# Two gated state-space convolutions on one core: the last two blocks' final sums taken apart, one accumulation moved into TensorE, and a new order table

## The chip, the cores and the metric

The kernel runs on one core of a Trainium2 chip. Its five engines work at the same time, each through its own queue of instructions: TensorE (PE) multiplies matrices into eight PSUM banks, VectorE (DVE) and ScalarE (ACT) work on elements and read PSUM, GpSimd (POOL) works on elements in SBUF and issues DMAs, SyncE (SP) only issues DMAs. An instruction waits on semaphores for what it needs, and all that stand behind it in its queue wait with it. The metric is the time of one execution on the device in microseconds (us); less is better.

## The reference

For an input `u` of 2048 positions and 512 channels, two independent state-space layers A and B each build a convolution kernel of 2048 taps per channel from 128 complex modes, convolve `u` with it, and a gate mixes the two results.

```python
def _A_ref(u, log_A_real, A_imag, C_real, C_imag, log_dt, D_skip):
    dt = jnp.exp(log_dt)
    A = -jnp.exp(log_A_real) + 1j * A_imag
    C = (C_real + 1j * C_imag) * dt[:, None]
    P = jnp.exp((A * dt[:, None])[:, :, None] * pos[None, None, :])
    K = 2.0 * jnp.einsum("dn,dnl->dl", C, P).real
    Kf = jnp.fft.rfft(K, L2)
    Uf = jnp.fft.rfft(u_t, L2)
    y = jnp.fft.irfft(Uf * Kf[None, :, :], L2)[:, :, :L]
    return y + u * D_skip[None, None, :]
...
g = _sigmoid((x * gate_w).sum(-1, keepdims=True))
return g * a + (1 - g) * b
```

All is computed in float32 here, with float16 pairs for the phases alone.

## The kernel before

**Units and blocks.** The 512 channels of A and B together make 64 units of 16 channel rows. A unit `u` builds its taps. PE adds up phases (`phase`, L508: eight float16 products, the only ones whose weights are loaded by instructions of their own); ACT takes sines and cosines; POOL multiplies powers of the decay (`grid0`, `grid1`, L524); DVE multiplies both (`cos_minus` to `one_sin`, L547 to L567); PE sums over the modes (`modes`, L575: 32 products of 32x64, run as 64 products in the trace, since a float32 product is two there, each with a weight load before it). So a float32 product of the program costs four PE instructions. ACT and DVE store the taps as `ks` (`keep`, `skip`).

Four units make a block `b` (16 blocks, 0 to 15). Two units' taps go through a first small transform (`first_k`, L597) and ACT copies it into `xall` (`keep_x`, L604). Then the block has eight middle transforms (`s2`, L634), each followed by two DVE products with the input's spectrum `v` (`products`, L645). The first product stays in the block's own part of `xall`; the second lands in `t2`, a part of `xall` that all blocks share, with real and imaginary rows exchanged. Four DMAs on POOL's queue add `t2` to the block's part, halves of the partitions exchanged (`add_products`, L675). Then four inverse transforms (`inverse`, L685: four products with the 128x128 table `mi` each), which ACT copies into `z` (`keep_z`, L691).

**Final sums.** Four blocks are a group `sb`. When all four have their `z`, four final sums (`final`, L707) multiply it with the gated table `eg`: 64 products each, with 32 weight columns and 64 moving columns, 16 for each of the group's four blocks. A sum fills two PSUM banks; ACT (in the last group ACT and DVE) copies them out (L718), and SP sends each of the two to DRAM, 128 KB. The gate is formed once, early: four sums over channels (`gate`, L737), a sigmoid, and a product on `eg`.

**What sets the order.** All operations are recorded in a list `ops`; the table `ORDER` says in which order they are issued, and each engine is held to that order by dependencies. A second table, `SLOTS`, says which of the eight PSUM banks each result takes. Both were written out beforehand; no rule of the program decides anything. Since a bank must be read before it is written again, `SLOTS` adds waits of its own.

**The end.** Behind the last unit stand, on PE: the first transforms of block 15, its eight middle transforms, block 14's inverses, block 15's inverses (which need the accumulating DMAs), and the last group's four final sums.

Of the kernel before, what the change touches and what calls it, by code (L numbers as in the profile page):

```python
# [11 lines left out]
F32 = mybir.dt.float32  # L12
# [7 lines left out]
M = 32  # L20
Q = 64
# [165 lines left out]
]  # L187


# [773 lines left out]
```

## Time and profile before

| | |
|---|---|
| times of three runs | 508.79, 510.26, 770.3 us; median 510.26 |
| profiled execution | 509.48 us, its span 507.6 us |
| mean granted TensorE clock | 0.95 |
| PE, DVE, ACT, POOL busy | 86%, 79%, 79%, 66% of the span |
| PE instructions | 12144 products, 12144 weight loads |

The span runs from the first to the last instruction; the time of the same execution is 1.9 us longer. A row of the profile names the line, the engine, the operation and the tiles (written tile, arrow, read tiles); what stands in brackets at its end is how long the engine was idle ahead of it and what ended that. "issue" means that nothing the profile shows was waited for. PE's busy time is of pipelined products and is no measure of how well the array is used. Line numbers are those of the kernel before.

### The profile page before, as it was taken

The numbers are of one execution on the slowest core, as the hardware profiler recorded it, in microseconds if no ns is written. First come the engines' busy times: TensorE is split into PE (matmuls) and PEld (weight loads), VectorE is DVE, ScalarE is ACT, GpSimd is POOL, SyncE is SP. The second block draws the span as 40 slices with busy tenths as digits, with TensorE's granted clock in tenths as the row PEclk, the third lists the DMA queues.
The fourth block names the chain that finished last, engine by engine and source line by source line (L and its number), as shares of the span: only waits on it lengthen the run. The fifth ranks groups of instructions, "written<-read, shape, count | busy, mean of one in ns | idle before, by whom it ended". The sixth has DMA issues, their size and how long they took to land.

```text
span 507.6 us, 27312 instructions
## 1 busy us (share of the span) xinstructions
PE 437.3 (86%) x12144; PEld 354.7 (70%) x12144; DVE 398.5 (79%) x860; ACT 399.3 (79%) x801; POOL 335.0 (66%) x320
## 2 busy tenths in 40 slices
PE   5886799896989889998999898968998888986774
PEld 5763664665858667876788677847786767876774
DVE  6498695999989999998789898859699788872401
ACT  4798799895999999799997997869979596843220
POOL 1499989996999899677784856554729662622200
PEclk9998899998999999999999999989999999989755
DMA  4537829026260633246513723271607352445312
GB/s 128 182 114 197 301 90 226 7 54 137 46 147 4 128 96 65 45 81 146 107 23 74 173 44 67 76 153 32 142 4 149 87 87 54 76 109 90 72 40 76
DMA packets 31349, 49.87 MB, mean 98 GB/s; under 512 B 10112, under 2 KB 16768, under 8 KB 31232
## 3 DMA queue, kind: packets, MB, share of 16 engines
q1 hardware_dynamic: 26112, 31.35, 21.5%
q0 software_dynamic: 5120, 16.78, 19.9%
q8 instruction: 95, 1.56, 1.3%
q14 instruction: 22, 0.18, 0.1%
HBM read 17.18 MB, written 5.77 MB: 45 GB/s over the span
## 4 chain that ended last, share of the span: by engine, by line
PE 49%; ACT 15%; DVE 13%; issue 9%; POOL 8%; DMA 5%; DVEq 0%; SPq 0%; ACTq 0%; POOLq 0%
PE ps L634 15%; PE psi L685 9%; PE pk L575 7%; PE p0s L508 6%; PE pf L707 5%; PE ps L597 5%; POOL f L524 4%; DMA xall<-xall 3%; ACT xall L604 3%; DVE xall L645 2%; ACT z L691 2%; PE psu L597 2%; DVE f L563 2%; ACT p0c L514 2%; DVE f L547 1%
## 5 line engine op out<-in xcount | busy, mean ns | idle before, releaser
L524 POOL TENSOR_TENSOR f<-bas 128x1024 f32<-128x1024 f32 (+1 forms) x128 | 204.7, 1645 | 71.4 <-PE pk L575 43.9
L634 PE MATMUL ps<-xall,gk 128*64 128x64 f32 (+1 forms) x1728 | 115.9, 260 | 13.7 <-issue 7.4
L634 PEld LDWEIGHTS ps<-xall,gk 128*64 128x64 f32 (+1 forms) x1728 | 105.4, 164 | 27.1 <-issue 12.3
L645 DVE TENSOR_TENSOR xall<-ps,v 128x256 f32<-128x256 f32 x256 | 95.1, 416 | 26.7 <-PE ps L634 24.3
L675 POOL DMA_DIRECT2D xall<-xall x64 | 61.5, 1119 | 50.6 <-ACT z L691 16.9
L575 PE MATMUL pk<-f,f 128*32 128x64 f32 x4096 | 72.4, 222 | 10.8 <-issue 3.6
L685 PE MATMUL psi<-mi,xall 128*128 128x128 f32 x512 | 71.9, 292 | 5.7 <-DMA xall<-xall 2.5
L575 PEld LDWEIGHTS pk<-f,f 128*32 128x32 f32 x4096 | 62.3, 111 | 19.1 <-issue 11.8
L685 PEld LDWEIGHTS psi<-mi,xall 128*128 128x128 f32 x512 | 64.0, 200 | 15.3 <-ACT z L691 5.0
L551 DVE TENSOR_TENSOR f<-f,p0c 128x512 f32<-128x512 f32 x64 | 43.6, 682 | 17.0 <-ACT p0c L520 14.2
L691 ACT COPY z<-psi 128x512 f32<-128x512 f32 x64 | 37.3, 604 | 22.0 <-PE psi L685 21.8
L508 PE MATMUL p1s<-cph,ones 64*128 64x512 f16 x128 | 49.5, 387 | 3.4 <-DVE ks L585 1.4
L563 DVE TENSOR_TENSOR f<-f,p1c 128x512 f32<-128x512 f32 x64 | 43.7, 683 | 10.3 <-ACT p1c L520 8.6
L597 PE MATMUL ps<-w,ks 64*64 64x64 f32 x2048 | 41.4, 226 | 11.6 <-issue 4.8
L508 PE MATMUL p0s<-cph,ones 64*128 64x512 f16 x128 | 49.6, 388 | 1.2 <-DVE f L567 0.5
L597 PEld LDWEIGHTS ps<-w,ks 64*64 64x64 f32 x2048 | 35.9, 139 | 20.9 <-issue 7.2
L508 PE MATMUL p0s<-cph,rot 64*128 64x512 f16 x128 | 49.2, 385 | 0.5 <-issue 0.5
L508 PE MATMUL p1s<-cph,rot 64*128 64x512 f16 x128 | 49.1, 384 | 0.0
L567 DVE TENSOR_TENSOR f<-f,p1s 128x512 f32<-128x512 f32 x64 | 43.6, 682 | 2.8 <-ACT p1s L517 0.8
L604 ACT COPY xall<-ps 128x512 f32<-128x512 f32 x64 | 37.3, 611 | 10.8 <-PE ps L597 10.7
L547 DVE TENSOR_TENSOR f<-f,p0c 128x512 f32<-128x512 f32 x64 | 43.6, 682 | 2.3 <-ACT p0c L520 1.2
L559 DVE SCALAR_TENSOR_TENSOR f<-f,p0s 128x512 f32<-128x512 f32 x64 | 43.4, 681 | 1.8 <-ACT p0s L517 1.0
(121 smaller groups left out, 794.4 us busy)
## 6 DMA issues: line engine op xcount, KB each, us to landing
xall<-xall POOLq DMA_DIRECT2D x64, 256.0 KB, 5.2
v<-v SPq DMA_DIRECT2D x64, 128.0 KB, 3.8
uraw<-in_us SPq DMA_DIRECT2D x16, 256.0 KB, 4.9
z<-in_ut SPq DMA_DIRECT2D x16, 256.0 KB, 5.9
out_dram<-ot SPq DMA_DIRECT2D x32, 128.0 KB, 1.9
par<-in_par SPq DMA_DIRECT2D x8, 256.0 KB, 3.7
gk<-in_gk SPq DMA_DIRECT2D x4, 512.0 KB, 7.1
eg<-in_eg SPq DMA_DIRECT2D x4, 512.0 KB, 7.0
```

The lines of the kernel that those rows point to most:

```text
L508: PE.matmul(ps, w[h : h + 64], cph[h : h + 64, j], start=j == 0, stop=j == 3, tile_position=(h, 0))
L524: G.tensor_tensor(o.rearrange("p k (a b) -> p k a b", b=8), x[:, :, hi : hi + n].unsqueeze(3).to_broadcast([128, 16, n, 8]), x[:, :, lo : ...
L547: V.tensor_tensor(f0[:, 0, :, 0:32], f0[:, 1, :, 0:32], half(u, p0c[u], True), OP.mult)
L563: V.tensor_tensor(f[:, 0], f[:, 1], p1c[u], OP.mult)
L575: PE.matmul(pk[32 * kd : 32 * kd + 32, i, :], f1[:, p, 4 * i + kd, :], f0[:, p, 4 * i + kd, :], start=p == 1, stop=p == 0, tile_position=( ...
L597: PE.matmul(ps[h][64 * ri : 64 * ri + 64, n, :], x[r], w1[r, ri, r], start=True, stop=True, tile_position=(64 * h, 64 * ri),)
L604: S.copy(o, pxs[key][h])
L634: PE.matmul(ps[h : h + w, j, 0:n], gk[:, k, h : h + w], xall[:, x0:x1, 2 * k : 2 * k + 2], start=True, stop=True, tile_position=(0, h),)
L645: V.tensor_tensor(k.rearrange("p x (k t) -> p k x t", t=2), p2s[b, g][:, :, 0:64].rearrange("p k (x t) -> p k x t", t=2), vv.unsqueeze(3). ...
L675: G.dma_start(out=xk(b)[o, s], in_=t2[t, s], accum_op=OP.add)
L685: PE.matmul(ps[:, i, :], xk(b)[:, x : x + 2, :].rearrange("p x k -> p (x k)"), mi, start=True, stop=True)
L691: S.copy(z[:, :, d0 : d0 + 4], pis[b, g].rearrange("p i r -> p r i"))
```

## The change

1. **The last group's final sums are split.** `final` for the last group now takes the first two of its blocks alone (12 and 13; 32 moving columns instead of 64), so it can stand before the last blocks are done. The last two blocks (14 and 15) get sums of their own, `last`: two of them, 64 products each, with 64 weight columns (two positions at once) and 64 moving columns (the same two positions). Of each 64x64 result only the two quarters where the positions agree are read. `eg` is laid out with the position next to the column for that.
2. **Copies and outputs follow.** `last_keep` copies each bank in four pieces of 32 partitions, on ACT and on DVE; the last group's outputs have a layout of their own (`out_at`) that the host code puts back in place.
3. **Block 15 has no accumulating DMAs.** Its `inverse` multiplies its own part of `xall` with `mi` and the shared part `t2` with `mt`, a copy of `mi` with the two halves of its rows exchanged, and adds both in PSUM: eight products instead of four.
4. **Eight unread products** (`hold`): 128x512, written to a bank that nobody reads.
5. **`ORDER` and `SLOTS` are other tables**, from the first entries to the last.

```diff
-    0, 19, 20, 21, 22, 23, 1, 2, 24, 45, 26, 25, 28, 29, 27, 30, 40, 41, 5, 74, 75, 32, 31, 78,
...
+    2480, 2493, 2483, 2481, 2482, 2477,
...
+    mt = const.tile([128, 128], F32, name="mt")
...
-    eg = const.tile([128, Q, 2, M], F32, name="eg")
+    eg = const.tile([128, 2, Q, M], F32, name="eg")
...
+    def hold(n):
+        PE.matmul(bank("pw"), ident, gk[:, 0:4, :].rearrange("p k x -> p (k x)"), start=True, stop=True)
...
     def inverse(b, g):
         pis[b, g] = ps = bank("psi", (128, 4, 128))
         for i in range(4):
             x = 2 * (4 * g + i)
-            PE.matmul(
-                ps[:, i, :], xk(b)[:, x : x + 2, :].rearrange("p x k -> p (x k)"), mi, start=True, stop=True
-            )
+            parts = [(xk(b), mi), (t2, mt)] if b == nblk - 1 else [(xk(b), mi)]
+            for n, (t, w) in enumerate(parts):
+                PE.matmul(
+                    ps[:, i, :], t[:, x : x + 2, :].rearrange("p x k -> p (x k)"), w,
+                    start=n == 0, stop=n == len(parts) - 1,
+                )
...
     def final(sb, j):
-        z0 = 0 if sb % 2 == 0 else NB
-        ps = [bank(f"pf{dp}")[:, 0:256].rearrange("p (a b) -> p a b", a=4) for dp in range(2)]
+        z0 = 0 if sb % 2 == 0 else 3 * NB if sb == nsb - 1 else NB
+        w = 32 if sb == nsb - 1 else 64
+        ps = [bank(f"pf{dp}")[:, 0 : 4 * w].rearrange("p (a b) -> p a b", a=4) for dp in range(2)]
...
+    def last(i):
+        ps = [bank(f"pl{dp}").rearrange("p (a q b) -> p a q b", a=8, q=2) for dp in range(2)]
+        for r4 in range(8):
+            for n in range(2):
+                for h in range(2):
+                    r = 32 * i + 4 * r4 + 2 * h
+                    for dp in range(2):
+                        rows = slice(64 * dp, 64 * dp + 64)
+                        PE.matmul(
+                            ps[dp][64 * h : 64 * h + 64, r4], eg[rows, n, r : r + 2, :],
+                            z[rows, 64 * n + r : 64 * n + r + 2, NB : 3 * NB],
+                            start=n == 0, stop=n == 1, tile_position=(64 * dp, 64 * h),
+                        )
+        pfs[i] = ps
+
+    def last_keep(i, dp):
+        ots[i, dp] = work.tile([128, 256], F32, name="ot", tag="ot", bufs=4)
+        o = ots[i, dp].rearrange("p (a b) -> p a b", a=8)
+        copy = V.tensor_copy if dp else S.copy
+        for rq in range(4):
+            rows = slice(32 * rq, 32 * rq + 32)
+            copy(o[rows], pfs[i][dp][rows, :, rq % 2])
...
-        if b >= 0:
+        if 0 <= b < nblk - 1:
             for h in range(2):
                 for x in range(2):
                     op("ya", add_products, b, h, x)
...
+    for h in range(2):
+        op("lm", dma, mt[64 * h : 64 * h + 64], a["mi"][64 - 64 * h : 128 - 64 * h])
...
-            if b % 4 == 3:
+            if b % 4 == (1 if b // 4 == nsb - 1 else 3):
...
+    for n in range(8):
+        op("wt", hold, n)
+    for i in range(2):
+        op("fl", last, i)
+        for dp in range(2):
+            op("fm", last_keep, i, dp)
+            op("fn", last_out, i, dp)
```

The end of the order on PE, before. `ps` is a middle transform's bank, `psi` an inverse's, `pf` a final sum's; a final sum is 64 rows, of which the first two and the last two stand here, and the three sums between them are left out.

```order
L634 MATMUL ps_9160<-xall,gk 64x64 x8
L634 MATMUL ps_9169<-xall,gk 64x64 x8
L685 MATMUL psi<-mi,xall 128x128 x32
L707 MATMUL pf_9240<-z,eg 32x64
L707 MATMUL pf_9241<-z,eg 32x64
...
L707 MATMUL pf_9456<-z,eg 32x64
L707 MATMUL pf_9457<-z,eg 32x64
L959 UNCONDITIONAL_BRANCH
```

The same place in the change, from the end of block 15's last inverse on (`mi` and `mt` in turn), with `pw` the unread bank and `pl` the last sums:

```order
L694 MATMUL psi<-mi,xall 128x128
L694 MATMUL psi<-mt,xall 128x128
L293 MATMUL pw<-gk,ident 128x512
L750 MATMUL pl_9548<-z,eg 64x64
L750 MATMUL pl_9549<-z,eg 64x64
...
L750 MATMUL pl_9627<-z,eg 64x64
L750 MATMUL pl_9628<-z,eg 64x64
L293 MATMUL pw<-gk,ident 128x512 x5
L1018 UNCONDITIONAL_BRANCH
```

All four inverses of block 15 stood together with block 14's (32 products in one row) ahead of four final sums; now two last sums follow the last inverse, one unread product stands between, and five stand behind everything. The other two unread products stand further ahead, one behind a final sum of the third group and one behind the last unit's phases.

The copies on ACT tell how inverses and early final sums alternate. `z` is the copy of an inverse, `ot` that of a final sum. Before:

```order
L604 COPY xall<-ps_9052 128x8x64
L718 COPY ot<-pf_8880 128x256
L691 COPY z<-psi 128x128x4 x11
L718 COPY ot<-pf_9240 128x256
L718 COPY ot<-pf_9309 128x256
L718 COPY ot<-pf_9384 128x256
L718 COPY ot<-pf_9456 128x256
```

In the change:

```order
L701 COPY z<-psi 128x128x4 x3
L733 COPY ot<-pf_9300 128x128
L733 COPY ot<-pf_9301 128x128
L701 COPY z<-psi 128x128x4 x2
L733 COPY ot<-pf_9382 128x128
L733 COPY ot<-pf_9383 128x128
L701 COPY z<-psi 128x128x4
L733 COPY ot<-pf_9463 128x128
L701 COPY z<-psi 128x128x4
L733 COPY ot<-pf_9464 128x128
L763 COPY ot<-pl_9548 32x256 x4
L763 COPY ot<-pl_9627 32x256 x4
```

Eleven inverses in a row and then the sums have become rounds of an early sum's two copies and one or two inverses' copies. On POOL the program ended with eight accumulating DMAs, for blocks 14 and 15:

```order
L524 TENSOR_TENSOR f_8747<-bas 128x512
L524 TENSOR_TENSOR f_8799<-bas 128x512
L524 TENSOR_TENSOR f_8854<-bas 128x1024
L675 DMA xall<-xall 64x1024 x8
L959 UNCONDITIONAL_BRANCH
```

Now the same place has four, those of block 14:

```order
L530 TENSOR_TENSOR f_8703<-bas 128x512
L530 TENSOR_TENSOR f_8764<-bas 128x512
L530 TENSOR_TENSOR f_8882<-bas 128x1024
L681 DMA xall<-xall 64x1024 x4
L1018 UNCONDITIONAL_BRANCH
```

More of the change, by code (lines that the diff above doesn't have):

```diff
@@ L707, in final @@
                         PE.matmul(
-                            ps[dp][32 * rq : 32 * rq + 32, r4, :], eg[rows, r, n, :],
-                            z[rows, 64 * n + r, z0 : z0 + 64],
+                            ps[dp][32 * rq : 32 * rq + 32, r4, :], eg[rows, n, r, :],
+                            z[rows, 64 * n + r, z0 : z0 + w],
                             start=n == 0, stop=n == 1, tile_position=(64 * dp, 32 * rq),
@@ L713, in final, with out_at, last_out @@
             pfs[sb, j, dp] = ps[dp]
+    def out_at(i, w):
+        o = out[nsb - 1].rearrange("j d p c -> (j d p c)")
+        return o[128 * i : 128 * (i + w)].rearrange("(p c) -> p c", p=128)
     def final_keep(sb, j, dp):
         ots[sb, j, dp] = work.tile([128, 256], F32, name="ot", tag="ot", bufs=4)
-        copy = V.tensor_copy if sb == nsb - 1 and dp else S.copy
-        copy(ots[sb, j, dp], pfs[sb, j, dp].rearrange("p a b -> p (a b)"))
+        w = 128 if sb == nsb - 1 else 256
+        S.copy(ots[sb, j, dp][:, 0:w], pfs[sb, j, dp].rearrange("p a b -> p (a b)"))
     def final_out(sb, j, dp):
-        dma(out[sb, j, dp], ots[sb, j, dp])
+        if sb == nsb - 1:
+            dma(out_at(128 * (2 * j + dp), 128), ots[sb, j, dp][:, 0:128])
+        else:
+            dma(out[sb, j, dp], ots[sb, j, dp])
+    def last(i):
[19 more added lines that the diff above has]
+            copy(o[rows], pfs[i][dp][rows, :, rq % 2])
+    def last_out(i, dp):
+        dma(out_at(1024 + 256 * (2 * i + dp), 256), ots[i, dp])
     psg = {}
@@ L744, in gate_e @@
     def gate_e(j):
-        e = eg[:, 16 * j : 16 * j + 16]
+        e = eg[:, :, 16 * j : 16 * j + 16]
         g = psg[j].rearrange("p (r m) -> p r m", m=M)
-        V.tensor_tensor(e, e, g.unsqueeze(2).to_broadcast([128, 16, 2, M]), OP.mult)
+        V.tensor_tensor(e, e, g.unsqueeze(1).to_broadcast([128, 2, 16, M]), OP.mult)
     def load_e(j):
-        dma(eg[:, 16 * j : 16 * j + 16], a["eg"][:, 16 * j : 16 * j + 16])
+        dma(eg[:, :, 16 * j : 16 * j + 16], a["eg"][:, :, 16 * j : 16 * j + 16])
     def batch(i):
@@ L913, in _layout @@
     ph = pi * (2 * k1[:, None, None] + 1) * l / 4096
-    eg = np.stack([np.cos(ph), -np.sin(ph)], 2) / 2048
+    eg = np.stack([np.cos(ph), -np.sin(ph)], 1) / 2048
     eg = np.tile(np.repeat(eg, 2, 0), (2, 1, 1, 1))
@@ L937, in _unlayout @@
 def _unlayout(o, nsb):
-    o = o.reshape(nsb, 4, 2, 4, M, 4, 64).transpose(4, 1, 5, 3, 0, 2, 6)
+    x = np.array(o).reshape(nsb, 8, 128, 4, 64)
+    y = x[nsb - 1].reshape(-1)
+    first = y[: 1024 * 128].reshape(4, 2, 128, 4, 32)
+    late = y[1024 * 128 :].reshape(2, 2, 128, 2, 4, 32).transpose(0, 3, 1, 2, 4, 5).reshape(4, 2, 128, 4, 32)
+    x[nsb - 1] = np.concatenate([late, first], -1).reshape(8, 128, 4, 64)
+    o = x.reshape(nsb, 4, 2, 4, M, 4, 64).transpose(4, 1, 5, 3, 0, 2, 6)
     o = np.array(o).reshape(M, 64, nsb, 2, 64)
```

16 lines of the change are left out of this document (8 added, 8 removed), and 305 rows, old and new, of the table ORDER.

## The prediction

> **What bounds the kernel now.** The page comes first (sections 1 and 2, then the chain), then who waited for whom, then the order of time in the last 50 us and the busy time by stages there.
>
> ```profile
> span 507.6 us, 27312 instructions
> PE 437.3 (86%) x12144; PEld 354.7 (70%) x12144; DVE 398.5 (79%) x860; ACT 399.3 (79%) x801; POOL 335.0 (66%) x320
> PEclk9998899998999999999999999989999999989755
> PE 49%; ACT 15%; DVE 13%; issue 9%; POOL 8%; DMA 5%; DVEq 0%; SPq 0%; ACTq 0%; POOLq 0%
> q8 instruction: 95, 1.56, 1.3%
> ```
>
> TensorE (PE) is the engine to follow: 86% busy, half of the chain, its clock full until the last two of the 40 slices. The chain also gives 9% to "issue", waits that no other engine explains. The last line names their cause. PE runs 12144 products and as many weight loads, 24288 instructions; 95 packets on the instruction queue make 24288 / 95 = 256 for each, 1.56 MB / 95 = 16 KB. PE's own program arrives in **pieces of 256 instructions**. In order of time, PE alone, in mid-run:
>
> ```profile
> 413.49 1.03 PE L597 MATMUL ps<-w,ks 64*64 64x64 f32 x51 [1.39 <-issue]
> 414.44 1.10 PE L575 MATMUL pk<-f,f 128*32 128x64 f32 x64
> 415.48 0.39 PE L508 MATMUL p0s<-cph,ones 64*128 64x512 f16 x1
> ...
> 416.44 0.30 PE L707 MATMUL pf<-z,eg 64*32 64x64 f32 x4
> 417.11 1.44 PE L707 MATMUL pf<-z,eg 64*32 64x64 f32 x124 [0.37 <-issue]
> 418.48 0.71 PE L634 MATMUL ps<-xall,gk 128*128 128x128 f32 x4
> 420.58 1.61 PE L634 MATMUL ps<-xall,gk 128*128 128x128 f32 x13 [1.39 <-issue]
> ```
>
> Between the second and third wait stand 124 + 4 = 128 products, so 256 instructions; they began 3.47 us apart. A piece whose work is shorter than the fetch of the next one ends in a wait. Over the run PE waited so (the four largest rows, and the largest of another kind):
>
> ```profile
> PE pf L707 <- issue: 8.9, 7, 2.9
> PE ps L634 <- issue: 7.4, 7, 1.9
> PE ps L597 <- issue: 4.8, 5, 2.8
> PE pk L575 <- issue: 3.6, 3, 2.0
> PE ps L597 <- DVE ks L585: 4.3, 2, 4.0
> ```
>
> The fetch waits add up to 24.7 us. Now the end, in order of time, all engines:
>
> ```profile
> 466.30 0.80 PE L597 MATMUL ps<-w,ks 64*64 64x64 f32 x36 [2.84 <-issue]
> 468.25 6.79 PE L634 MATMUL ps<-xall,gk 128*64 128x64 f32 x128 [1.16 <-ACT xall L604]
> 475.09 1.09 DVE L645 TENSOR_TENSOR xall<-ps,v 128x256 f32<-128x256 f32 x3 [0.16 <-PE ps L634]
> 476.86 3.31 POOL L675 DMA_DIRECT2D xall<-xall  x4 [16.89 <-ACT z L691]
> 482.25 3.75 PE L685 MATMUL psi<-mi,xall 128*128 128x128 f32 x16 [2.45 <-DMA xall<-xall]
> 486.68 3.79 PE L685 MATMUL psi<-mi,xall 128*128 128x128 f32 x16 [0.68 <-ACT z L691]
> 491.14 2.41 PE L707 MATMUL pf<-z,eg 64*32 64x64 f32 x152 [0.68 <-ACT z L691]
> 494.84 2.06 PE L707 MATMUL pf<-z,eg 64*32 64x64 f32 x128 [1.29 <-issue]
> 498.59 2.06 PE L707 MATMUL pf<-z,eg 64*32 64x64 f32 x128 [1.69 <-issue]
> 502.33 1.77 PE L707 MATMUL pf<-z,eg 64*32 64x64 f32 x104 [1.69 <-issue]
> 504.16 0.42 DVE L718 COPY ot<-pf 128x256 f32<-128x256 f32 x1 [3.26 <-PE pf L707]
> ```
>
> The last products of block 15 end at 476.2; its accumulating DMAs hold PE until 482.25; two pairs of inverse transforms follow at half clock, and four final sums that start 3.70 to 3.75 us apart though each is only 2.06 us of work. From the last copy's end (504.6) to the span's end are 3.0 us. I call 468.25, the start of block 15's middle transforms, T0: the span ends at T0 + 39.35. The clock by stages:
>
> ```profile
> 475.10:482.25 7.15, 4.03 (x32) 3.67 (x33) 1.07 (x3) 2.74 (x5) 3.31 (x4) 0.92 0.59 97
> 491.10:504.20 13.10, 8.30 (x512) 7.35 (x512) 1.32 (x4) 1.20 (x4) 0.00 (x0) 0.50 0.20 65
> ```
>
> The number behind the busy times is the granted clock. It is 0.92 in the stage of block 14's inverses and the DMA, where PE is busy 4.03 of 7.15 us, and 0.50 in the final sums, at 8.30 of 13.10: a share of about 60% doesn't bring it back once it is lost, and the wait at 482 lost it.
>
> The Trainium skill, "Runtime: NRT & Kernel Launch", section "Instruction fetch mechanics", also has blocks of 256 instructions, but calls the cost of crossing one mostly hidden. By that rule those four rows would be nothing; here they are 24.7 us, so the measurement decides.
>
> **The change, part by part.** The sum is made against the profiled execution: span 507.6, time 509.5 (the median of the three runs is 510.3).
>
> *The accumulation of block 15 goes.* Four DMAs on POOL's queue vanish, and with them 482.25 - 476.2 = 6.0 us of the chain. What is late next is not a transfer but PE itself. Behind T0 it has eight middle transforms, two inverses of block 14, the first early final sum, one more inverse of block 14, and only then block 15's inverse. In instructions: 256 + 32 + 256 + 16 = 560, or 2.2 pieces; at 3.75 us a piece 8.2 us. By work, these rows price a final sum, two inverses at full clock, and (1280 products in 58.6 us, so 128 in 5.9) the middle transforms:
>
> ```profile
> 455.06 1.48 PE L707 MATMUL pf<-z,eg 64*32 64x64 f32 x128
> 456.47 2.05 PE L685 MATMUL psi<-mi,xall 128*128 128x128 f32 x16
> L634 PE MATMUL ps<-xall,gk 128*64 128x64 f32 x1280 | 58.6, 254 | 10.0 <-issue 6.0 <-ACT xall L604 1.6 <-DMA gk<-in_gk 1.3
> ```
>
> So 5.9 + 2.05 + 1.48 + 1.03 is about 10.4 us: block 15's inverse starts at T0 + 10.4 instead of T0 + 14.0. This gain is 3.6 us, not 6.
>
> *Block 15's second terms by the exchanged table.* Each of its four inverses has 8 products instead of 4, so 32 instructions and 2.05 us at full clock (3.75 at half). They alternate with early final sums 1, 2 and 3, 256 instructions each: 288 a round, more than a piece, with 2.05 + 1.48 = 3.5 us of work. So the fetch paces each round at 3.75. I count the boundaries back from the program's end and get: first inverse done and next piece entered at T0 + 12.9, then three pieces of 3.75 to T0 + 24.1, the rest of the last inverse 1.2, its copy 0.7 beside the hold that stands there (about 0.9), so T0 + 26.2 for the last sums.
>
> *These last sums* are two groups of 256 instructions, where four stood. The 64x64 form costs as the first sums do (1.09 us for 64 in the chain's row below), 2.2 us a group; a boundary stands some 20 instructions before each group's end: T0 + 28.2 at the first, 3.75 later at the second, 0.2 for the rest. PE's last needed product ends at T0 + 32.2, against T0 + 35.9 before: 3.7 us.
>
> ```profile
> 437.78 1.09 PE ps L597 x64
> ```
>
> *Copies out.* Each of the last ones is split into four on 32 partitions, on ACT and on DVE side by side. A whole one took 0.42 us; no row shows a quarter, so one is between 0.1 and 0.42, four between 0.4 and 1.7; I take 1.7, since the free size per partition stays 256. With the 3.0 us from copy to end: T0 + 36.9.
>
> *Unread products.* Of eight, one stands in the copy's gap, two in the steady part, and **five behind the last sum**. Nobody waits for them, but the program ends when PE does. Their form, 128x512 in f32, has a neighbour in the gate sums: 32 instructions in 14.5 us is 0.45 apiece, 0.9 for a product of two; by the inverse (four products of 128 columns in 1.03 or 1.88 us) it is 1.03 or 1.88.
>
> ```profile
> L737 PE MATMUL psg<-z,small 128*128 128x512 f32 x32 | 14.5, 602 | 0.0
> ```
>
> Five cost 4.6 us at full clock and 9.4 at half. To close I allow 0.5 us, between nothing and the 3.0 - 1.9 = 1.1 that the old end takes beside an output's landing:
>
> ```profile
> out_dram<-ot SPq DMA_DIRECT2D x32, 128.0 KB, 1.9
> ```
>
> The end is T0 + 37.3 to T0 + 42.1, behind the output either way. No wait as long as the DMA's stands in the new tail, so the clock should come in full; the stall before the second group (1.5 in 3.75 us, 60% busy) may lose it or not. I take a third of the way, 38.9. **Tail: -0.4 us, from -2.0 to +2.8.**
>
> The Trainium skill, "TensorE: Matmul & The Clock Gate", Part 1, says that the clock is halved after an idle window of about 3.4 us and restored after a busy one. By that rule five products in a row would regain the full clock within them, about 8 us, an estimate from that page, and the end would be T0 + 40.7 from a cold start. The 0.50 of the final sums agrees with its first half; a return within such products no row here shows.
>
> *The new order.* The table is not only new in its last sixth: it differs from the first entries on. Before T0, 23050 of PE's instructions stand before and 23069 in the change. I cut both orders into pieces of 256 and price each by the rows above (a phase's eight products 416.44 - 415.48 = 0.96; the 128-wide middle transforms like inverses). Pieces that come out under 3.75 us fall short by 16.5 us in all before T0, and by 20.6 in the new order. The trace's own figure for the old one, the four rows less the 4.7 us in the tail, is 20.0, so the count catches most of it. Thus **+4.1 us** of fetch waits, of which a part will lie in waits for data: I take 3. The two holds in the steady part add 0 (in a wait) to 2.0; I take 0.5.
>
> The other engines' queues are reshuffled as well. ACT gets three more table loads:
>
> ```profile
> L520 ACT ACT_TABLE_LOAD x6 | 7.7, 1283 | 0.1
> 150.00:300.00 150.00, 139.74 (x4058) 114.15 (x4049) 136.92 (x297) 139.45 (x285) 116.54 (x115) 1.00 0.40 82
> sum 468.25, PE 410.59 PEld 329.94 DVE 390.78 ACT 391.67 POOL 331.72; mean PE 82.12 PEld 65.99 DVE 78.16 ACT 78.33 POOL 66.34
> ```
>
> (the second row is the stage from 150 to 300 us, the third the sum up to T0) 3 x 1.28 = 3.8 us on an engine busy 139.45 of 150 in the middle stage; over the whole it has 76 us of room. PE is idle before T0 in 468.25 - 410.6 = 57.7 us, some 37 of them in waits that aren't fetches. A different order can save or add some of these; no row prices that. From the nearest rows I bound it at a quarter, 9 us, on either side, and take 0.
>
> The exchanged table itself (two loads of half of `mi`), the laid-out `eg` (same 1024 elements per gate product) and the smaller output DMAs touch no wait: the loads stand some 1,500 steps into an order of 2,494, long before use, and an output lands in 1.9 us.
>
> Sum: 509.5 + 3 + 0.5 - 0.4 = **512.6**.
>
> **Rivals.** *The shorter chain counts* (chance 0.25). The holds run at full clock and end near the output (T0 + 37.3), and the reshuffle removes waits for data instead of adding fetches, two thirds of my bound: 509.5 - 2.0 - 6 = 501.5. For it: 37 us of such waits are there, single ones up to 4.0 us. Against: the shortfalls counted above.
>
> *Instructions don't bound it* (0.05). If a piece came in time, the last sums would end at T0 + 10.4 + 8.2 + 4.4 + 0.9 + 4.4 = T0 + 28.3 and the holds at T0 + 33.4; with no +3 the time is 509.5 - 6.0 = 503.5. The fetch rule cited above would give this. The rows at 494.84 to 502.33 speak against it.
>
> *The tail goes cold* (0.2). If the fetch waits between the early sums drop the clock as in the stage of 0.50, each inverse of block 15 takes 3.75 instead of 2.05 (four: +6.8, of which some 2 us lie in fetch waits), and the holds take 9.4 (T0 + 42.1, +3.2 over my value). With the full 4.5 before T0 (4.1 + 0.5, rounded): 509.5 - 0.4 + 4.8 + 3.2 + 4.5 = 521.6, slower. It decides once PE's idle share in a round passes some 40%, as in the final sums; at 3.5 of 3.75 us busy it should stay far below, so I give it no more.
>
> *That the change does what its words say* is partly refuted by the order alone: five of eight unread products lie in no wait, and the order is new throughout. Both are in the forecast.
>
> **How the numbers follow.** Forecast 0.5 (508 to 517), the quicker cases 0.3, cold 0.2. The unknown of the order alone, 9 us either way, widens all. The range 499 to 523 leaves out about a tenth below and a tenth above. Two per cent, about what a measurement of this kernel can tell from no change, is 10 us: faster 0.1 (from the quicker cases' lower half), slower 0.19 (most of the cold case), within 0.71.
>
> **What would show it.** Right: the same four fetch rows at 24 us before T0; T0 at 470 to 473; block 15's inverse about 10 us behind T0; last sums 3.75 us apart at their second piece; PE ending later than the last output's issue, with five products behind it. Wrong: T0 earlier than 465 (the order wins), a tail of under 36 us (fetch or clock better than counted), or a clock of 0.50 from the first early sum on.

## The result and the profile after

The changed kernel took **503.73 us** (median of four runs, 503.43 to 505.28), a ratio of **0.9892 [0.985, 0.9934]** to the kernel before; the same kernel in a later comparison gave 502.65 us and 0.984 [0.9774, 0.9906]. The prediction was 512.6 us and "same": the time went 1.1 to 1.6% the other way. (Executions more than 1.5% above the fastest of the same kernel are left out of all ratios, which leaves two of six for `no_end_again` and three of twelve for `changed_shift64`, and the profiles of these two, of `oldbody_newtail` and of `exchange_14_15` fell on such long executions, so that their sums say less than their single waits.)

The page of the changed kernel (line numbers are now its own): span, busy times, granted clock, chain, and the packets of PE's program:

```profile
span 501.8 us, 27909 instructions
PE 441.3 (88%) x12448; PEld 355.1 (71%) x12448; DVE 395.0 (79%) x864; ACT 406.1 (81%) x816; POOL 332.5 (66%) x316
PEclk9999998999999999999999999999999999998899
PE 45%; DVE 13%; ACT 12%; issue 10%; POOL 10%; DMA 8%; SPq 1%; DVEq 0%; ACTq 0%; POOLq 0%
q8 instruction: 97, 1.59, 1.3%
```

PE has 4.0 us more work in a span that is 5.8 us shorter, and its clock is full from 468.2 us to the end (half from 461.4 to 468.2). Its end in order of time, from the wait ahead of T0 (the start of block 15's middle transforms) on:

```profile
462.67 1.34 PE L603 MATMUL ps<-w,ks 64*64 64x64 f32 x37 [4.16 <-issue]
465.94 5.62 PE L640 MATMUL ps<-xall,gk 128*64 128x64 f32 x128
475.92 0.39 PE L694 MATMUL psi<-mt,xall 128*128 128x128 f32 x2
477.57 1.29 PE L718 MATMUL pf<-z,eg 64*32 64x32 f32 x128
480.77 1.51 PE L718 MATMUL pf<-z,eg 64*32 64x32 f32 x128
484.20 0.27 PE L718 MATMUL pf<-z,eg 64*32 64x32 f32 x8
488.41 0.49 PE L694 MATMUL psi<-mi,xall 128*128 128x128 f32 x2 [1.43 <-issue]
490.36 3.89 PE L750 MATMUL pl<-z,eg 64*64 64x64 f32 x246
495.63 0.44 PE L750 MATMUL pl<-z,eg 64*64 64x64 f32 x10 [1.38 <-issue]
496.00 4.84 PE L293 MATMUL pw<-gk,ident 128*128 128x512 f32 x10
496.09 1.49 ACT L763 COPY ot<-pl 32x256 f32<-32x256 f32 x4 [1.98 <-issue]
496.16 1.72 DVE L763 COPY ot<-pl 32x256 f32<-32x256 f32 x4 [1.75 <-issue]
475.45 22.96 SPq L256 DMA_DIRECT2D out_dram<-ot  x13
```

T0 is 465.94 (468.25 before) and the span ends 35.86 us behind it (39.34 before): by these two profiles 2.3 us came from ahead of T0 and 3.5 from the tail. The experiments show that this division is an accident of the two executions.

Who waited for whom, on PE ahead of T0, the rows that end in "issue" (us in total, times, longest), in the changed kernel; they add up to 20.2 us with a row of 0.2:

```profile
PE pk L581 <- issue: 10.3, 10, 3.0
PE ps L603 <- issue: 4.9, 2, 4.2
PE psi L694 <- issue: 2.9, 3, 1.6
PE pf L718 <- issue: 1.9, 3, 1.4
```

The same view of the kernel before, cut at its T0, gives 22.7 us: the rows of L634, L597 and L575 shown in the prediction, and these:

```profile
PE pf L707 <- issue: 4.3, 4, 2.9
...
PE p1s L508 <- issue: 1.1, 1, 1.1
PE psi L685 <- issue: 1.0, 1, 1.0
PE p0s L508 <- issue: 0.5, 1, 0.5
```

These waits moved to other lines (the taps' sums instead of middle transforms and final sums) and did not grow by 4 us; they fell.

### The profile page after: what moved, and what is told of

The parts are those of the page before. It is cut to its first block, busy times and chain, and to the rows that moved or that the text cites. A ratio compares the mean times of both kernels' runs of the same rounds, so it can differ in the third digit from the quotient of the medians.

```text
span 501.8 us, 27909 instructions
## 1 busy us (share of the span) xinstructions
PE 441.3 (88%) x12448; PEld 355.1 (71%) x12448; DVE 395.0 (79%) x864; ACT 406.1 (81%) x816; POOL 332.5 (66%) x316
## 4 chain that ended last, share of the span: by engine, by line
PE 45%; DVE 13%; ACT 12%; issue 10%; POOL 10%; DMA 8%; SPq 1%; DVEq 0%; ACTq 0%; POOLq 0%
PE ps L640 12%; PE psi L694 10%; PE pk L581 6%; PE p0s L514 5%; POOL f L530 4%; PE pf L718 4%; DMA xall<-xall 4%; PE ps L603 3%; DVE xall L651 3%; DMA v<-v 2%; ACT xall L610 2%; PE psu L603 2%; PE pw L293 2%; DVE f L565 2%; DVE f L561 1%
## 5 line engine op out<-in xcount | busy, mean ns | idle before, releaser
L530 POOL TENSOR_TENSOR f<-bas 128x512 f32<-128x512 f32 (+1 forms) x128 | 204.1, 1653 | 69.0 <-PE pk L581 51.9
L640 PE MATMUL ps<-xall,gk 128*64 128x64 f32 (+1 forms) x1728 | 113.2, 253 | 4.4 <-DVE xall L651 0.9
L640 PEld LDWEIGHTS ps<-xall,gk 128*64 128x64 f32 (+1 forms) x1728 | 102.4, 155 | 17.6 <-issue 2.0
L581 PE MATMUL pk<-f,f 128*32 128x64 f32 x4096 | 74.2, 221 | 17.7 <-issue 10.3
L681 POOL DMA_DIRECT2D xall<-xall x60 | 59.2, 1164 | 24.8 <-PE p0s L514 6.3
L694 PEld LDWEIGHTS psi<-mi,xall 128*128 128x128 f32 x512 | 62.6, 193 | 16.1 <-issue 7.2
L603 PEld LDWEIGHTS ps<-w,ks 64*64 64x64 f32 x2048 | 34.0, 136 | 22.1 <-DVE ks L591 12.3
L603 PE MATMUL ps<-w,ks 64*64 64x64 f32 x2048 | 38.9, 223 | 11.8 <-DVE ks L591 5.8
```

What stands on the lines that cost most here:

```text
L530: G.tensor_tensor(o.rearrange("p k (a b) -> p k a b", b=8), x[:, :, hi : hi + n].unsqueeze(3).to_broadcast([128, 16, n, 8]), x[:, :, lo : ...
L581: PE.matmul(pk[32 * kd : 32 * kd + 32, i, :], f1[:, p, 4 * i + kd, :], f0[:, p, 4 * i + kd, :], start=p == 1, stop=p == 0, tile_position=( ...
L603: PE.matmul(ps[h][64 * ri : 64 * ri + 64, n, :], x[r], w1[r, ri, r], start=True, stop=True, tile_position=(64 * h, 64 * ri),)
L640: PE.matmul(ps[h : h + w, j, 0:n], gk[:, k, h : h + w], xall[:, x0:x1, 2 * k : 2 * k + 2], start=True, stop=True, tile_position=(0, h),)
L681: G.dma_start(out=xk(b)[o, s], in_=t2[t, s], accum_op=OP.add)
L694: PE.matmul(ps[:, i, :], t[:, x : x + 2, :].rearrange("p x k -> p (x k)"), w, start=n == 0, stop=n == len(parts) - 1,)
```

## The experiments

**1. The order apart from the end.** `newbody_oldtail`: the kernel before, with the new `ORDER` and `SLOTS` up to T0 and its old end.

```diff
-    0, 19, 20, 21, 22, 23, 1, 2, 24, 45, 26, 25, 28, 29, 27, 30, 40, 41, 5, 74, 75, 32, 31, 78,
+    0, 1, 40, 19, 20, 21, 22, 23, 24, 26, 25, 28, 74, 27, 29, 30, 5, 31, 75, 32,
...
```

> The new order up to block 15's middle transforms, then the old end: accumulating DMAs for block 15, four final sums over all four blocks, no unread products. Only the body differs from the kernel before. Theory A (the two traces' split: the body saves 2.3 us, the tail 3.5): 509.5 - 2.3 = 507.2, ratio about 0.995. Theory B (the order does most of it): 505 or less, ratio 0.991 or less. The prediction's own term for the body, +3.5: 513, ratio 1.007.

`oldbody_newtail`: the changed kernel with the old order up to T0, the new end behind it, and no unread products ahead of T0 (six of the eight are left).

```diff
-    0, 1, 40, 19, 20, 21, 22, 23, 24, 26, 25, 28, 74, 27, 29, 30, 5, 31, 75, 32, 41, 33, 42, 34,
+    0, 19, 20, 21, 22, 23, 1, 2, 24, 45, 26, 25, 28, 29, 27, 30, 40, 41, 5, 74,
...
```

> The old order up to block 15's middle transforms, then the new end: split final sums, exchanged table for block 15, six of the eight unread products (the two that stood in the body are left out). Only the tail differs from the kernel before. Theory A: 509.5 - 3.5 = 506.0, ratio about 0.993. Theory B: 508 to 509.5, ratio 0.997 or more. The prediction's own term for the tail, -0.4: 509.1, ratio 0.999.

Measured: **0.9834 [0.9787, 0.988]** for the new order with the old end, **1.0013 [0.9978, 1.0048]** for the old order with the new end. The order carries the whole gain, the new end on the old order none that shows. So theory B holds, and the prediction's own term for the tail; theory A and the +3.5 for the body are out. The old end in the new order, PE in order of time:

```profile
479.97 5.94 PE L656 MATMUL psi<-mi,xall 128*128 128x128 f32 x32 [4.80 <-DMA xall<-xall]
486.59 1.75 PE L678 MATMUL pf<-z,eg 64*32 64x64 f32 x154 [0.68 <-ACT z L662]
490.00 1.47 PE L678 MATMUL pf<-z,eg 64*32 64x64 f32 x128 [1.66 <-issue]
493.47 1.58 PE L678 MATMUL pf<-z,eg 64*32 64x64 f32 x128 [2.00 <-issue]
496.94 1.73 PE L678 MATMUL pf<-z,eg 64*32 64x64 f32 x102 [1.89 <-issue]
```

Here 32 inverse instructions take 5.94 us, not 7.54, and the sums start 3.41 to 3.47 us apart. From T0 (467.33) to the span's end are 34.8 us. Over the profiles with the old end that tail is 34.0 to 37.8 us in seven of eight, and 39.3 in the one that the prediction had; with the new end and its five last products it is 34.4 to 36.7 in seven. Before's profile had half the clock for the last 26 us of its span, the others with the old end for at most 19 us behind T0.

**2. The five products at the end.** `no_end_products`: the changed kernel without the five unread products behind the last sum.

```diff
-    for n in range(8):
+    for n in (0, 2, 3):
         op("wt", hold, n)
```

> The changed kernel without the five unread products behind the last sum. Theory A: the output's end stands right behind them (last copy ends at 497.9 of the trace, plus the 3.0 us that the kernel before took from copy to end, is 500.9 against 501.8), so 0.5 to 1 us quicker: 502.8 to 503.2. Rival, the prediction's step that the program ends with PE and they cost what stands behind the last sum: 4 us quicker, 499.7. If they somehow help, slower than 503.7.

`no_end_again` is the same kernel on another chip; `no_unread_products` leaves out all eight.

> The changed kernel without the five unread products behind the last sum, once more, beside the others on one chip. Both theories: 0.975 to 0.985.

> The changed kernel without all eight unread products. Beside the kernel without the five at the end (0.980 and 0.972): if the two in the steady part and the one in the copy's gap cost what their PE time is, 0.97 us each, 0.3 to 0.6% less again, 0.967 to 0.977; if they lie in waits, or hold up the clock, the same or a little more, 0.972 to 0.985.

Measured: 0.9797 [0.9743, 0.985], 0.9719 [0.9624, 0.9814], and without all eight 0.9778 [0.964, 0.9917]. The last sum of `no_end_products`, in order of time:

```profile
490.12 0.44 PE L721 MATMUL pl<-z,eg 64*64 64x64 f32 x10 [1.70 <-issue]
```

It ends at 490.56 and the span at 495.29, 4.73 us later; in the changed kernel it is 496.07 and 501.80, 5.73 us. So these two traces show 1.0 us for the five products; the rest of their 4.84 us lies beside copies and output. The ratios lie 0.4 to 1.7% under those of the changed kernel, more than 1.0 us is; their intervals overlap, so the difference isn't settled. (0.9719 rests on two executions; the median of all six, 500.06 us, is 0.979 of 510.56.) By its time alone, 499.68 us, `no_end_products` meets the rival's 499.7 and not theory A's 502.8 to 503.2. But in its profile T0 came at 460.93, 5.0 us earlier than in the changed kernel's, and the five stand behind T0: most of what that execution gained isn't theirs. The three unread products further ahead cost nothing that shows.

**3. Block 15's accumulating DMAs back.** `accumulate_15`: the changed kernel, whose block 15 has its four DMAs again and four products an inverse instead of eight.

```diff
-            parts = [(xk(b), mi), (t2, mt)] if b == nblk - 1 else [(xk(b), mi)]
+            parts = [(xk(b), mi), (t2, mt)] if b == nblk else [(xk(b), mi)]
...
-        if 0 <= b < nblk - 1:
+        if b >= 0:
```

> The changed kernel with block 15's four accumulating DMAs back, right behind its last product, and four products for each of its inverses again. Theory A: the inverse starts about 6 us behind the last product (474.8) instead of 0.9, +5.1, less up to 1 us for the shorter rounds, and up to 3 more if the clock drops in the wait: 508 to 511. Rival (PE has other work then, and the DMAs were hidden): 504.

Measured 0.991 [0.9875, 0.9944]. PE waits 5.82 us for the DMAs, and the tail is 39.2 us, 3.3 more than in the changed kernel:

```profile
479.31 2.04 PE L665 MATMUL psi<-mi,xall 128*128 128x128 f32 x8 [5.82 <-DMA xall<-xall]
```

Between the two ratios 0.2 to 0.7% are left of that, with intervals that overlap: the direction agrees, the size isn't told. The time, 505.7 us, lies between theory A's 508 to 511 and the rival's 504.

**4. The order by halves, and a filled wait.** Beside a repeat of the changed kernel, the old end with the new order in the last sixth alone, or in the first five sixths alone; and the kernel before with two unread 128x512 products in PE's wait for block 15's DMAs.

> The changed kernel itself once more, on the chip of the three others, as their measure. All theories: ratio 0.985 to 0.993 as found before, about 504 us.

```diff
-    2138, 2144, 2122, 2123, 2139, 2145, 2149, 1888, 2048, 2051, 2049, 2052, 2150, 2152, 2153,
+    2123, 2139, 2145, 2149, 1888, 1326, 1333, 1891, 2105, 2104, 1895, 1896, 1893, 1894, 1897, 1899, 1900, 1898, 2048, 2050,
...
```

> The kernel before with the new order in the last sixth alone, up to block 15's middle transforms (five sixths and the end stay old; the edits are left out). Theory C (the order's gain is made by what stands close ahead of the end, and by the end then meeting a warm clock): nearly all of the 0.983 that the new order gave with the old end, so 0.983 to 0.989. Theory D (it is made along the whole run): 0.994 to 1.0.

> The kernel before with the new order in the first five sixths alone; the last sixth and the end are old. Theory C: 0.996 to 1.002, since the old end is cold again. Theory D: 0.983 to 0.990.

```diff
+    for n in range(2):
+        op("wt", hold, n)
```

> The kernel before with one thing added: two unread products of 128x512 between block 14's last inverse and block 15's first, in PE's wait for the accumulating DMAs. Theory E (the old end is long because that wait halves the clock): the clock stays full, four inverses take 2.05 us a pair instead of 3.75, 3.4 us quicker, ratio 0.993. Rival (the clock falls anyway, or the final sums at 3.5 to 3.75 us apart set the end alone): 0.998 to 1.002.

Measured: 0.9971 [0.993, 1.0012] and 0.9939 [0.9902, 0.9975] for the two parts of the order; neither gives the whole of 0.9834, which both have together. Theory D holds for the last sixth; for the first five sixths the value lies between the two theories. The filled wait gave 0.9977 [0.9938, 1.0017]: no gain that shows. Its trace shows what theory E said of the clock, full until 495.3 us, with block 15's inverses at 1.97 and 2.02 us a pair:

```profile
486.37 2.02 PE L659 MATMUL psi<-mi,xall 128*128 128x128 f32 x16 [1.06 <-DMA xall<-xall]
```

So unread work in that wait kept the clock. But its tail, 34.0 us, is little under the 34.8 to 37.8 of the old ends without it: the 39.3 of the kernel before's profile was no usual cost to be won back.

**5. The same orders with other piece boundaries.** What an order changes without changing any work is where PE's pieces of 256 instructions end. So both kernels were shifted: one early group of unread warm-up products (8 wide ones, 32 PE instructions) became 24, 40 or 56 small ones (96, 160, 224 instructions), about 21 us from the start. Every later boundary falls 64, 128 or 192 instructions further on in the same work. The time is not quite the same, as the expectations below have it: in the kernel before the small ones take 2.96, 4.83 and 6.69 us, the group that they replace 1.9. The first sum over the modes (`pk`), at 29.67 us there, starts at 29.70, 31.53 and 34.25 us; the changed kernel is 0.3, 1.2 and 3.4 us late at such a place (32.22 us). So only a shift of 64 costs nothing by itself.

```diff
     def warm_up(n):
         pw = bank("pw")
+        if n == 1:
+            for i in range(40):
+                PE.matmul(pw[0:64, 0:64], ident[0:64, 0:64], ident[0:64, 0:64], start=True, stop=True)
+            return
```

> The kernel before, in which one of the early groups of unread warm-up products is written as 40 small ones (64x64) in place of 8 wide ones: 128 more PE instructions near 21 us, about the same time, so that every later boundary between pieces of 256 instructions falls half a piece further on in the same work. Nothing else moves, and the order is the same. Theory (the order gains because the fetch of a next piece stands behind data transfers, and another order lets other boundaries meet transfers): the fetch waits ahead of the middle transforms of block 15, 22.7 us in the profile before, change by 3 us or more either way, and the ratio leaves 0.995 to 1.005. Rival (the order gains by its waits for data and its banks): boundaries are neutral, 0.997 to 1.004.

> The changed kernel with the same 128 instructions more at its start. Theory (boundaries against transfers): the fetch waits ahead of the middle transforms of block 15, 17.0 to 21.6 us in the profiles of the new order, rise or fall by 3 us or more, and the gain of 1.1 to 1.6% is partly gone or grows: outside 0.983 to 0.990. Rival (the waits for data in the order): 0.984 to 0.989 again.

> The kernel before with 64 more PE instructions at its start (24 small warm-up products in place of 8 wide ones): boundaries a quarter of a piece further on. First reading (where the boundaries meet the transfers decides, and neither order is better in itself): the fetch waits ahead of the middle transforms of block 15 lie anywhere from 17 to 32 us, and the ratio follows them, 0.99 to 1.02. Second reading (the new order is better by about 1% wherever the boundaries lie): this one stands 0.8% or more behind the changed kernel with the same shift.

> The changed kernel with the same 64 instructions more. First reading: 0.98 to 1.015, and its distance to the kernel before with the same shift is not the 1.1 to 1.6% of no shift (at 128 instructions it was 0.1%). Second reading: 0.8% or more ahead of it.

> The kernel before with 192 more PE instructions at its start (56 small products in place of 8 wide ones): three quarters of a piece. First reading: fetch waits from 17 to 32 us, 0.99 to 1.02. Second reading: 0.8% or more behind the changed kernel with the same shift.

> The changed kernel with the same 192 instructions more. First reading: 0.98 to 1.015, no fixed distance to the kernel before with the same shift. Second reading: 0.8% or more ahead of it.

The fetch waits of the kernel before with a shift of 64, PE ahead of T0 (they and a row of 0.6 add up to 36.0 us):

```profile
PE pk L579 <- issue: 15.2, 10, 3.5
PE pf L711 <- issue: 9.1, 4, 5.1
PE ps L638 <- issue: 7.7, 5, 2.7
...
PE psi L689 <- issue: 3.4, 3, 1.8
```

All eight, with T0 and the sum of PE's "issue" waits ahead of it from the same view, and of its other waits:

| shift | before: ratio | T0 | issue | other | changed: ratio | T0 | issue | other |
|---|---|---|---|---|---|---|---|---|
| 0 | 1 | 468.3 | 22.7 | 32.9 | 0.989, 0.984 | 465.9, 463.7 | 20.2, 15.3 | 35.1, 36.5 |
| 64 | 1.0318 [1.0252, 1.0383] | 487.4 | 36.0 | 29.8 | 0.993 [0.9849, 1.001] | 478.9 | 25.5 | 35.1 |
| 128 | 1.0167 [1.0111, 1.0222] | 477.8 | 30.4 | 31.9 | 1.0153 [1.009, 1.0215] | 475.7 | 27.2 | 30.4 |
| 192 | 1.0114 [1.003, 1.0198] | 476.1 | 26.7 | 29.6 | 1.0007 [0.9951, 1.0063] | 473.8 | 24.1 | 33.3 |

A shift of 64 costs the kernel before 3.2%, one of 128 the changed kernel 2.6 to 3.1% (0.2% of it the longer warm-up), and the fetch waits rise with it; waits for data do not. "Boundaries are neutral" is out. Both kernels are quickest unshifted, though the changed one at 64 lies within the intervals, and of the 5.8 us that 192 costs the kernel before up to 4.6 can be warm-up. The distance between the orders is 1.1 to 1.6, 3.8 (2.7 by the medians of all executions), 0.1 and 1.1%. So the gain is partly the order's and partly the place's. The first reading missed 64 in the kernel before (1.02 and 32 us were its upper ends), the second missed 128. (The expectations have 17.0 to 21.6 us of fetch waits for the new order; the view used here gives 15.0 to 20.2 over the five profiles listed further below.)

The shift of 64 moved T0 by 19.1 us: 13.3 more in fetch waits, 3.1 less in others, and 9.0 in the rest, which is PE's work with its clock. The granted clock stands behind the busy times, 0.98 in the kernel before and 0.96 with the shift:

```profile
30.00:468.25 438.25, 388.72 (x11106) 310.23 (x11095) 373.26 (x779) 371.52 (x752) 319.40 (x300) 0.98 0.44 97
30.00:487.40 457.40, 395.50 (x11109) 315.44 (x11098) 373.85 (x779) 372.77 (x752) 319.61 (x300) 0.96 0.42 93
```

In the trace's record of the clock that is half the clock for 17.9 and 36.2 us ahead of T0, and half of the difference is 9.1 us. A stretch of half clock starts within 2 us of the end of each fetch wait of 1.7 us or more, four in the kernel before and seven with the shift (in the changed kernel at one of two). By these traces a late fetch can cost more than its wait.

**6. What makes a fetch late.** The trace has each fetch's start. In the kernel before, between 30 us and T0, the next piece's fetch began 1.16 us (median of 87) behind the entry into a piece, took some 1 us, and PE could go on 1.2 to 1.6 us behind its end: 3.3 to 3.75 us in all where nothing was late. But 26 of 87 began more than 1.6 us behind it, and of 22.7 us of waits at boundaries 15.8 stand behind fourteen of those.

The late ones go with data transfers. At 39 of the 87 entries the DMA engines were less than 10% busy with data in the 1.16 us behind the entry: the fetch began 1.04 us behind it in the median, never more than 2.5, and the waits are 3.0 us. At 33 they were at least 60% busy: median 1.80, nine over 2.5, and 17.2 us of waits. Over all twenty profiles the median is 0.99 us at 738 quiet entries, 2.03 at 259 where POOL's queue alone was that busy, and 1.53 at 235 with SP's alone (31 of the quiet ones began over 2.5 us late all the same). Two examples, each with the transfers between the entry and the fetch (queue: packets, MB, share of 16 engines) and the PE row behind. In the kernel before, entry 46.78, fetch at 51.27, loads from SP:

```profile
q1 hardware_dynamic: 560, 1.29, 90.5%
...
53.77 1.39 PE L575 MATMUL pk<-f,f 128*32 128x64 f32 x63 [2.04 <-issue]
```

In the changed kernel, entry 454.19, fetch at 460.24, with block 14's accumulating DMAs on POOL's queue; the PE row is the first of the tail shown above, with its wait of 4.16 us:

```profile
q0 software_dynamic: 255, 0.80, 81.8%
```

`exchange_14_15` takes those DMAs away: block 14's second terms go through `mt` as well, block 15's lie in another part of `xall`, and seven of eight unread products are left out.

```diff
-            x0 = 32
+            x0 = 96 if b == nblk - 1 else 32
...
+            if b >= nblk - 2:
+                parts.append((xall[:, 96:128] if b == nblk - 1 else t2, mt))
...
-        if 0 <= b < nblk - 1:
+        if 0 <= b < nblk - 2:
```

> The changed kernel without seven of the eight unread products and with block 14's second terms by the exchanged table too (16 more products in its inverses; block 15's second terms lie in another part of xall so that both stand). Block 14's four accumulating DMAs are gone. Theory (they hold up the next piece's fetch): the fetch that began 4.4 to 6 us behind its piece's entry near 460 us begins about 1 us behind it, and the 2.5 to 4.2 us fetch wait there goes; against that stand 16 products of 0.26 us, 4.1 us of PE. Beside the kernel without the end products: -1% to +0.3%, so 0.970 to 0.983. Rival (the accumulating DMAs don't delay the fetch): the late start stays, and it is 2 to 4 us slower than the kernel without the end products, 0.984 to 0.99.

Measured 0.9805 [0.9742, 0.9867], inside the theory's range, with an interval that reaches into the rival's. At the same place (entry 461.60) the fetch began at 463.62, with nothing under way:

```profile
q1 hardware_dynamic: 1, 0.00, 0.0%
...
466.04 0.70 PE L574 MATMUL ps<-w,ks 64*64 64x64 f32 x33 [0.15 <-issue]
```

In the eight profiles of the new order that keep block 14's DMAs the fetch there began 3.20 to 6.48 us behind the entry and PE waited 1.29 to 4.49 us; without them both lie below all eight. Beside 0.9797 and 0.9719 without the end products no gain shows in the time, as 16 more products of PE stand against it. That 2.03 us passed there without data says that transfers aren't the only cause of a late start.

`more_transfers` adds four unread transfers of 1 MB on SP's queue:

```diff
+            if sb == 2 and dp:
+                spare = nc.dram_tensor(f"spare{j}", (128, 2048), F32).ap()
+                dma(spare, gk[:, 0:16].rearrange("p k x -> p (k x)"))
```

> The changed kernel with four more transfers of 1 MB that nobody reads (part of gk to a spare place in DRAM), each issued by SP right behind an output of the third group, between about 320 and 460 us. PE gets no work and no wait from them. First reading (a piece's fetch stands behind data transfers): each of them lasts 4 to 6 us and covers a piece's entry or two, so three or more fetches between 320 and 460 us begin 3 us or more behind their piece's entry while that transfer runs; fetch waits ahead of block 15's middle transforms 4 to 12 us more than in the changed kernel (17.0 to 21.6), ratio 0.995 to 1.012. Rival (fetches don't stand behind data): the fetch waits stay within 2 us; what the loads on the same queue lose shows as waits for data, ratio 0.985 to 0.995.

Measured 0.9899 [0.9853, 0.9946], fetch waits 21.9 us. Two of the four transfers ran while POOL's queue moved nothing: during one (415.0 to 419.2 us) the entry at 418.24 had its fetch 0.72 us behind it, during the other (427.4 to 432.6) the entry at 430.11 had it 1.63 us behind, and PE waited at neither boundary that followed. So "three or more" was wrong. The other two met block 14's DMAs and the same entry, here 457.48: the fetch began at 463.96, 6.48 us behind, and PE waited 4.46 us:

```profile
q0 software_dynamic: 163, 0.52, 51.1%
q1 hardware_dynamic: 276, 1.17, 50.3%
...
466.31 0.92 PE L603 MATMUL ps<-w,ks 64*64 64x64 f32 x25 [4.46 <-issue]
```

6.05 us in the changed kernel's profile, 4.41 in its repeat, 6.48 here: this doesn't separate SP's transfers from POOL's. The ratio lies in the rival's range, and its interval ends below the first reading's 0.995. So four more megabytes on SP's queue cost nothing that shows; how strongly its transfers hold a fetch up, next to POOL's, stays open.

## Why the prediction was wrong, step by step

**What bounds the kernel: right.** PE and the fetch of its pieces. The shifts show it more strongly than the profile of before could: with one early warm-up group rewritten, T0 moved from 468 to 487 us.

**The new order, +3 us: the step that failed.** The prediction priced each piece by its work, set every fetch at 3.75 us, and counted a shortfall of 16.5 us before and 20.6 after. It took the nearness of 16.5 to the measured 20.0 (22.7 with the smaller rows) for proof. But about 14 of these 22.7 us stand at thirteen pieces with 3.75 us of work or more, whose fetch began late; the match was chance. The piece's time isn't a constant: in the repeat of the changed kernel the shortest starts lie 2.6 to 3.2 us apart, where the fetch came early, and a wait of 4.2 us stands in the result's profile where it came late. Over the profiles with the new order at no shift (changed, its repeat, experiments 1 to 3; fetch waits 20.2, 15.3, 15.0, 15.2, 17.8) the mean is 16.7 us, over the old order (before, the filled wait) 22.8: **-6.1 instead of +3**. The other waits rose from 33.2 to 36.6, +3.4 inside the bound of 9; the rest ahead of T0, PE's work with its clock, fell by 2.5. T0 came 5.2 us earlier, 464.4 against 469.6. The ratio of 0.9834 is 8.5 us of 510, with an interval from 6.1 to 10.9. How much of it lies in an old end that keeps its clock longer no run separates.

The Trainium skill, "Runtime: NRT & Kernel Launch", section "Instruction fetch mechanics", has the next block fetched while the present one runs, and calls the crossing mostly hidden. The first half agrees with the traces, one piece ahead; the second doesn't, by 15 to 36 us. The Trainium skill, "DMA: Bandwidth & Descriptors", section "Queues, rings and completion order", says that a DMA engine takes turns among its queues packet by packet, and that a packet is some 9 to 17 descriptors. By that a fetch would stand behind about one packet. The profile's page has what it counts as packets of POOL's queue:

```profile
q0 software_dynamic: 4800, 15.73, 18.8%
```

0.188 x 16 x 501.8 / 4800 is 0.31 us for one; the fetch at 460.24 began some 4.9 us later than the usual 1.16. If one of these is a packet in the Trainium skill's sense, turns among queues don't explain the delay. If each is one descriptor, 9 to 17 of them are 2.8 to 5.3 us, an estimate with that section's count, and turns would explain it. No run tells which, nor whether the fetch stands in the DMA engine or its request ahead of it.

**Two unread products in the steady part, +0.5: not seen.** Leaving out all eight gave nothing beyond the five.

**The tail, -0.4: right as a sum, by steps that were partly off.** On the old order the new end is worth +0.7 us (1.0013; -1.1 to +2.5), inside -2.0 to +2.8. In the changed kernel's profile:

- Block 15's inverse starts at about 475.7, T0 + 9.8 (10.4 predicted): right.
- Rounds start 3.20 and 3.43 us apart (3.75): a boundary in them costs 0.2 us or less, and only the last waits 1.43. The last sums start at T0 + 24.4 (26.2) and end at T0 + 30.1 (32.2).
- Four quarter copies take 1.72 us on DVE, as taken. Without the five products the span ends 4.73 us behind the last sum; 1.7 + 3.0 had been counted.
- The five products run at full clock, 4.84 us, not at the 6.2 between warm and cold; the program ends 0.96 behind PE (0.5). PE ends behind the last output's issue (498.41), as said.

So this tail is 35.86, not 38.9: 2.1 in the pace, 1.4 in the clock, less 0.5 at the end. It didn't make the gain, because the 39.35 it was set against was the longest of eight. A term worked against one execution carried that execution's accident.

**The rivals.** "The shorter chain counts" named the right side and the time (501.5), and the holds did run at full clock, but its main reason was wrong, a reshuffle that removes waits for data: these grew. "Instructions don't bound it" came to 503.5, beside 503.73 measured: that is luck, for the shifts refute it. "The tail goes cold" didn't happen, and its sign, an idle share of some 40%, is not borne out: in `newbody_oldtail` the sum at 490.00 is 1.47 us of work in 3.47, 58% idle, and the clock stayed full until 494.7 us. What was to show the prediction wrong came about: a tail under 36 us, and T0 earlier than 465 in three of these five profiles, though not in the result's (465.94).

**The quickest version.** The changed kernel without its last five products has the lowest ratios measured, 0.9797 and 0.9719. That it beats the changed kernel itself is not shown, since the intervals overlap.

## What to carry to other kernels

Where one engine runs thousands of short instructions, look at where its program's pieces end before trusting any change of order: count the waits at every 256th instruction, see how far behind the entry each fetch began and which transfers run then. Shift the boundaries by some unread instructions as a control; here this alone was worth up to 3%, more than the change. A count that agrees with a measured total is no proof until it agrees place by place.

## What the runs showed that was not expected

- A fetch of 16 KB began up to 6.5 us behind the entry into the piece before it (in the places shown), 1.16 us in the median; with the accumulating DMAs gone from that place 2.03 us.
- Of the waits at the boundaries of the kernel before, 17.2 of 22.7 us stand where the DMA engines were at least 60% busy with data just behind the entry.
- 64 more PE instructions at the start made the kernel before 3.2% slower (16 us), its fetch waits 13 us longer, and its stretches at half clock ahead of T0 18 us longer.
- T0 of programs with the same order up to it lay between 460.9 and 467.3 us, so one profile doesn't measure 1%.
- The old final sums are not always cold: 1.47 to 1.75 us of work apiece in one profile, 2.06 in another.
